# A recurrent attention block and its feed-forward layer: two rounds by halves of the features, and one product by seven for eight twice

## The chip, the cores and the metric

The kernel runs on one core of a Trainium2 chip. The metric is device time in microseconds (us), the median of several runs. All data are 32-bit floats, except that the two weight matrices arrive as 64-bit floats.

## The reference

```
# x: 8 batches x 8 heads x 512 tokens x 64;  state: 8 x 8 x 32 x 64
scores  = x @ state^T / 8 ;  a  = softmax(scores) ;  xread = a  @ state     # per batch and head
scores2 = state @ x^T / 8 ;  a2 = softmax(scores2);  sread = a2 @ x
t = concat([xread, sread], tokens)         # 4352 rows (8 x 544) x 512 features (8 heads x 64)
h = t @ w_in                               # 512 x 2048
g = h * erf(softplus(h))
out = g @ w_out                            # 2048 x 512
```

## The kernel before

**Attention.** Each of the 8 batches has an attention: scores of 512 tokens against 32 states, both softmaxes, with 32x32 turns on DVE. The weights of tokens are turned through 16 small DMAs from SBUF to SBUF (`send`, L360: `sc<-xT`), and the product `read_tokens` (L275) gives the states' reading of the tokens. `xread` is never formed: the states are multiplied with `w_in` first (`mixed_pair`, L383: `h<-w_in,st`), and the hidden layer is the product of that with the softmax weights `aT`.

**Products by seven for eight.** Both large products are cut in 2 x 2 blocks and made by seven block products instead of eight, with sums of blocks on DVE ahead of them and of results behind. `hidden_wide` (L469 to L520) makes the hidden layer of one batch in passes of 256 columns (L489); its results leave PSUM through copies on ACT and sums on DVE. `project_wide` (L620 to L667) makes the second product (L641), 256 columns a pass. Batch 0 is an exception: its products are plain, 512 columns wide (L919 and L926), while the weights are still arriving and are being turned from 64-bit to 32-bit floats on ACT and DVE (`weight`, L143 to L175).

**Order.** After batch 0, the loop at the end of the kernel takes batches 1 to 7, and for each two steps `u`, one per half of the 2048 features. In each step the second product of what the step before made runs between the pieces of the hidden product. `w_in` lies in SBUF by halves; the other half comes back from a copy in DRAM (`bring`, L1108, 2 MB a batch). The first half's output goes out by plain stores on the SP queue (L706), the second half's is added in DRAM by accumulating stores on POOL's queue (L704). The 256 rows of states come last (`hidden_states`, L534: 128 columns a pass; `project7`, L616; `store7`). The order of batch 0 and the start is a list of names (`order0`); after it, the order in which the code issues things. `in_order` (L81) then binds each engine to that order.

Of the kernel before, what the change touches and what calls it, by code (L numbers as in the profile page):

```python
# [15 lines left out]

@with_exitstack
def kernel(
# [8 lines left out]

# [8 lines left out]
    NF = d_ff // P  # L44
    GF = 4
    NG = NF // GF
    TB = S + Ns
    scale = 1.0 / (D ** 0.5)
    assert NI * Ns == P and 2 * D == P and d_model == H * D and S == 512 and NI == NK
    assert (B * Ns) % P == 0 and B * Ns <= S  # L50

    const = ctx.enter_context(tc.tile_pool(name="const", bufs=1))
    xin = ctx.enter_context(tc.tile_pool(name="xin", bufs=1))
    att = ctx.enter_context(tc.tile_pool(name="att", bufs=1))
    small = ctx.enter_context(tc.tile_pool(name="small", bufs=2))
    keep = ctx.enter_context(tc.tile_pool(name="keep", bufs=2))
    mix = ctx.enter_context(tc.tile_pool(name="mix", bufs=4))
    act = ctx.enter_context(tc.tile_pool(name="act", bufs=2))
    outs = ctx.enter_context(tc.tile_pool(name="outs", bufs=2))
    ps_at = ctx.enter_context(tc.tile_pool(name="ps_at", bufs=2, space=PSUM))  # L60
    ps_h = ctx.enter_context(tc.tile_pool(name="ps_h", bufs=2, space=PSUM))
    ps_o = ctx.enter_context(tc.tile_pool(name="ps_o", bufs=1, space=PSUM))

    ident = const.tile([P, P], F32, name="ident")
    make_identity(nc, ident)

    ring = const.tile([P, 2, 3, GF, GF, P], F32, name="ring")
    dram = ctx.enter_context(tc.tile_pool(name="dram", bufs=1, space=bass.MemoryType.DRAM))
    x_t = {}


    def load_x(b):
        t = xin.tile([P, NC, H, D], F32, name="x")
        for h in range(H):
            nc.sync.dma_start(out=t[:, :, h, :], in_=x[b, h].rearrange("(c p) d -> p c d", p=P))
        x_t[b] = t

    def traced():
        return len(nc.cur_bb.bb.instructions)

    def in_order(begun, engines=(nc.tensor, nc.vector, nc.scalar, nc.sync)):  # L81

        last = {}
        for i in nc.cur_bb.bb.instructions[begun:]:
            if i.engine in last:
                tc.add_manual_dep(i, last[i.engine].name, mybir.DependencyInfo(
                    mybir.DependencyClass.NoSync, mybir.DependencyReason.DATA), reason="in_order")
            if i.engine in [e.engine for e in engines]:
                last[i.engine] = i

    begun = traced()

    xq_t = {}

    def load_xq(b, hs=range(H)):
        if b not in xq_t:
            xq_t[b] = xin.tile([P, NI, S // Ns, Ns], F32, name="xq")
        t = xq_t[b]  # L100
        for h in hs:
            i, e = h // 2, h % 2
            for k in range(2):
                nc.sync.dma_start(
                    out=t[D * e + Ns * k:D * e + Ns * k + Ns, i],
                    in_=x[b, h, :, Ns * k:Ns * k + Ns].rearrange("(m t) d -> t m d", t=Ns))


    st = const.tile([P, B, P], F32, name="st")
    away0 = ring[:, 1, 0].rearrange("p k i t -> p (k i t)")  # L110
    st0 = away0[:, 512:640].rearrange("p (g d) -> p g d", g=2)
    x0 = xin.tile([P, NC, H, D], F32, name="x").rearrange("p c h d -> p (c h d)").rearrange(
        "p (h c d) -> p h c d", h=H, c=NC)
    x_t[0] = x0.rearrange("p h c d -> p c h d")
    for i in range(NI):
        (nc.scalar, nc.sync)[i % 2].dma_start(
            out=x0[:, 2 * i:2 * i + 2].rearrange("p h c d -> p h (c d)"),
            in_=x[0, 2 * i:2 * i + 2].rearrange("h (p c) d -> p h (c d)", c=NC))
        if i == 1:
            nc.sync.dma_start(out=st0, in_=state[0].rearrange("(g h) n d -> (h n) g d", g=2))  # L120

    def load_st(hs):
        for h in hs:
            i, e = h // 2, h % 2
            nc.sync.dma_start(out=st[Ns * i:Ns * i + Ns, 1:B, D * e:D * e + D],
                              in_=state[1:B, h].rearrange("b n d -> n b d"))


    w_in = const.tile([P, NF // 2, NK, P], F32, name="w_in")
    away = ring[:, :, 2].rearrange("p u k i t -> p u (k i t)").rearrange(  # L130
        "p u (j k f) -> p u j k f", k=NK, f=P)
    of_group = [w_in[:, GF * g:GF * g + GF] for g in range(2)] + [away[:, u] for u in range(2)]
    pieces_in = [of_group[j // 2][:, 2 * (j % 2):2 * (j % 2) + 2] for j in range(NF // 2)]
    kept_in = dram.tile([2, P, NF // 2, NK * P], F32, name="kept_in")
    w_out = const.tile([P, NF, d_model], F32, name="w_out")

    fetched = []

    def weight(dst, src, parts=1):

        flat = lambda t: t.rearrange("p a b c -> p (a b c)" if len(t.shape) == 4 else
                                     "p a b -> p (a b)")
        if src.dtype == F32:
            fetched.append(nc.sync.dma_start(out=dst, in_=src))
            return [lambda: None] * 2 * parts, [lambda: None] * 3 * parts
        raw = act.tile([P, 2 * 2 * d_model], U32, name="raw", bufs=3)  # L150
        blocks = [(raw, src)]
        if len(src.shape) == 4:
            blocks = [(raw.rearrange("p (h x) -> p h x", h=2)[:, h], src[:, h]) for h in range(2)]
        for to, part in blocks:
            part = part.bitcast(U32)
            fetched.append(nc.sync.dma_start(
                out=to.rearrange("p (a b) -> p a b", a=part.shape[1]), in_=part))
        n, m = dst.shape[1] // parts, d_model // parts * 4
        on_act, on_dve = [], []
        for k in range(parts):  # L160
            to, words = dst[:, n * k:n * k + n], raw[:, m * k:m * k + m]
            words = words.rearrange("p (n w) -> p n w", w=2)
            lo, hi, to = words[:, :, 0], words[:, :, 1], flat(to)
            d = to.bitcast(U32)
            on_act += [
                lambda to=to, hi=hi: nc.scalar.activation(out=to, in_=hi.bitcast(F32),
                                                          func=ACTF.Copy, scale=2.0 ** -112),
                lambda lo=lo: nc.scalar.activation(out=lo, in_=lo, func=ACTF.Copy,
                                                   scale=2.0 ** -29)]
            on_dve += [  # L170
                lambda d=d: nc.vector.tensor_scalar(d, d, 3, None, op0=ALU.logical_shift_left),
                lambda on=nc.vector, d=d, lo=lo: on.tensor_tensor(d, d, lo, op=ALU.add),
                lambda d=d, hi=hi: nc.vector.scalar_tensor_tensor(
                    out=d, in0=hi, scalar=0x80000000, in1=d, op0=ALU.bitwise_and,
                    op1=ALU.bitwise_or)]  # L175
        return on_act, on_dve

    gw = GF * P

    def weights_in(j):  # L180
        return weight(pieces_in[j], moe_w_in[:, 2 * P * j:2 * P * j + 2 * P].rearrange(
            "(k p) (h f) -> p h k f", p=P, f=P), 2 if j == 0 else 1)

    def weights_out(j):
        return weight(w_out[:, 2 * j:2 * j + 2, :],
                      moe_w_out[2 * P * j:2 * P * j + 2 * P].rearrange("(t p) e -> p t e", p=P))

    leads = [0]

    def warm(out, n, by=ident):  # L190
        for _ in range(n):
            nc.tensor.matmul(out=out, lhsT=by, rhs=by, start=True, stop=True)

    def lead(out):

        warm(out, leads[0])
        leads[0] = 0

    sT = const.tile([P, NK, 2, Ns, B // 2], F32, name="sT")
    st00 = away0[:, 768:1024]  # L200
    where = {h: (g, q) for g, hs in enumerate(((0, 2, 1, 3), (5, 7, 4, 6)))
             for q, h in enumerate(hs)}
    aT = {}

    def all_of(jobs):
        for f in jobs:
            f()

    over = lambda t: t.unsqueeze(2).to_broadcast([P, NC * NI, Ns])

    def inverse(z):
        nc.vector.tensor_scalar(z, z, 1e-9, None, op0=ALU.add)
        nc.vector.reciprocal(z, z)

    marks = []

    def scored(b, xT, pool=ps_at, names=("at", "at")):


        s2 = [pool.tile([P, S], F32, name=name) for name in names]  # L220
# [8 lines left out]
    def scores(b, xT, *pool):  # L229
# [3 lines left out]
        for e in range(2):  # L233
            last = nc.scalar.copy(sc[:, e], s2[e])
# [30 lines left out]
    def read_tokens(b, a2T, z2, pool=ps_at, name="at"):  # L265
# [14 lines left out]
        if z2 is None:  # L280
            return lambda on: on(sn, sr)
# [1042 lines left out]
```

## Time and profile before

| | |
|---|---|
| median of 3 runs | 722.42 us (721.96 to 723.0) |
| span of the profiled execution | 720.8 us |
| that execution's own time | not given apart from its span; the median stands 1.6 us above the span |
| PE busy | 714.0 us, 99% |
| DVE busy | 489.0 us, 68% |
| ACT busy | 420.9 us, 58% |
| DMA moved | 74.65 MB, mean 104 GB/s |
| share of PE in the chain that ended last | 97% |

The profile has one execution of the program. PE is TensorE's matmuls, PEld its weight loads, DVE is VectorE, ACT ScalarE, POOL GpSimd, SP SyncE; a `q` behind an engine is its DMA queue. A group's line has source line, engine, operation, what is written and read, shapes, count, busy us and mean ns of one, and the idle time of the engine ahead of it. L numbers are lines of the kernel before.

### The profile page before, as it was taken

Reading aid. Unit: us, or ns where it says so; the run is one execution under the profiler, and the core shown is the slowest. Engines: PE = TensorE matmul, PEld = TensorE weight load, DVE = VectorE, ACT = ScalarE, POOL = GpSimd, SP = SyncE. Lnnn points to the kernel's source line nnn. Section 1 sums busy time; section 2 is a strip of 40 time slices with the busy share of each in tenths; the row PEclk is TensorE's granted clock in tenths of the full one; section 3 lists DMA queues with packets and bytes.
Section 4 is the critical chain, followed back from the end, with each engine's and each line's share of the span. In section 5 each row is a group of like instructions: output and inputs, shape, how many; then the busy total and the mean of one; then the engine's idle time right before and its main releaser. Section 6 shows DMA issues by size and latency. Waiting matters only on the chain.

```text
span 720.8 us, 10926 instructions
## 1 busy us (share of the span) xinstructions
PE 714.0 (99%) x4291; PEld 558.4 (77%) x4291; DVE 489.0 (68%) x796; ACT 420.9 (58%) x619; POOL 25.2 (3%) x34
## 2 busy tenths in 40 slices
PE   8999999999999999999999999999999999999997
PEld 7444347688878878787888878787888888889996
DVE  6998886869767875768575766577575736555533
ACT  4999897657474627564566547472666545452340
POOL 0000000000100000000000000000000000000000
PEclk9999999999999999999999999999999999999999
DMA  8879686650348172514523280615142322002100
GB/s 253 238 206 245 220 239 192 152 156 30 56 93 205 26 145 35 163 34 107 77 43 136 58 146 0 176 31 148 29 121 67 100 35 30 31 29 30 22 9 30
DMA packets 144068, 74.65 MB, mean 104 GB/s; under 512 B 123024, under 2 KB 132624, under 8 KB 142480
## 3 DMA queue, kind: packets, MB, share of 16 engines
q1 hardware_dynamic: 139152, 65.89, 33.6%
q0 software_dynamic: 4032, 7.34, 7.6%
q8 instruction: 34, 0.56, 0.3%
q10 hardware_dynamic: 832, 0.72, 0.3%
q14 instruction: 18, 0.15, 0.1%
HBM read 49.81 MB, written 20.45 MB: 97 GB/s over the span
## 4 chain that ended last, share of the span: by engine, by line
PE 97%; DMA 2%; ACT 0%; issue 0%; SPq 0%; DVE 0%
PE o L641 47%; PE h L489 17%; PE o L926 8%; PE at L489 7%; PE h L534 3%; PE o L616 3%; PE at L919 2%; PE h L919 2%; PE h L383 2%; DMA raw<-in_moe_w_out_dram 2%; PE at L383 2%; PE at L275 1%; PE o L224 1%; PE at L908 1%; DMA x<-in_x_dram 1%; PE at L1018 0%
## 5 line engine op out<-in xcount | busy, mean ns | idle before, releaser
L641 PE MATMUL o<-w_out,ring 128*128 128x256 f32 x896 | 203.0, 379 | 0.0
L641 PEld LDWEIGHTS o<-w_out,ring 128*128 128x128 f32 x896 | 169.8, 190 | 24.9 <-DVE ring L1127 0.8
L641 PE MATMUL o<-raw,ring 128*128 128x256 f32 x672 | 161.4, 381 | 0.0
L641 PEld LDWEIGHTS o<-raw,ring 128*128 128x128 f32 x672 | 126.5, 190 | 25.9 <-ACT m L385 9.2
L472 DVE TENSOR_TENSOR ring<-ring,at 128x512 f32<-128x512 f32 x56 | 38.2, 682 | 86.6 <-ACT ring L510 79.5
L482 ACT ACTIVATE ring<-ring 128x512 f32<-128x512 f32 x112 | 70.6, 631 | 20.1 <-DVE ring L472 19.1
L489 PE MATMUL h<-aT,m 128*128 128x256 f32 x336 | 81.8, 379 | 0.0
L1127 DVE TENSOR_TENSOR ring<-ring 128x1024 f32<-128x1024 f32 (+1 forms) x61 | 70.7, 1201 | 4.5 <-ACT ring L546 4.5
L489 PEld LDWEIGHTS h<-aT,m 128*128 128x128 f32 x336 | 63.8, 190 | 10.0 <-issue 1.2
L926 PE MATMUL o<-w_out,ring 128*128 128x512 f32 x128 | 59.5, 599 | 0.0
L626 DVE TENSOR_TENSOR ot<-uv,o 128x256 f32<-128x256 f32 (+1 forms) x56 | 31.0, 553 | 37.7 <-PE o L641 35.9
L664 ACT COPY ot<-o 128x256 f32<-128x256 f32 x28 | 10.4, 372 | 77.9 <-PE o L641 77.9
L704 POOL DMA_DIRECT2D out_dram<-ot x28 | 24.5, 943 | 656.6 <-DVE ot L626 557.0
L926 PEld LDWEIGHTS o<-w_out,ring 128*128 128x128 f32 x128 | 23.7, 190 | 28.1 <-issue 26.6
L626 DVE TENSOR_TENSOR ot<-ot,o 128x256 f32<-128x256 f32 x56 | 22.1, 416 | 27.8 <-ACT ot L664 27.7
L673 DVE TENSOR_TENSOR ring<-ring 128x512 f32<-128x512 f32 x56 | 38.6, 689 | 1.4
L674 DVE TENSOR_TENSOR ring<-ring 128x512 f32<-128x512 f32 x56 | 36.1, 684 | 0.0
L385 ACT COPY m<-h 128x512 f32<-128x512 f32 x13 | 7.6, 586 | 46.3 <-PE h L383 46.1
L506 ACT COPY ring<-h 128x512 f32<-128x512 f32 x28 | 16.4, 585 | 29.6 <-PE h L489 29.6
L501 ACT COPY ring<-h 128x512 f32<-128x512 f32 x28 | 16.4, 586 | 28.0 <-PE h L489 25.5
L489 PE MATMUL h<-sy,m 128*128 128x256 f32 x112 | 31.0, 399 | 0.0
L489 PE MATMUL h<-sy,sx 128*128 128x256 f32 x112 | 30.9, 398 | 0.0
(205 smaller groups left out, 994.9 us busy)
## 6 DMA issues: line engine op xcount, KB each, us to landing
w_in<-kept_in SPq DMA_DIRECT2D x7, 2048.0 KB, 8.8
out_dram<-ot SPq DMA_DIRECT2D x33, 256.0 KB, 2.2
raw<-in_moe_w_in_dram SPq DMA_DIRECT2D x16, 512.0 KB, 5.4
raw<-in_moe_w_out_dram SPq DMA_DIRECT2D x8, 1024.0 KB, 5.8
xq<-in_x_dram SPq DMA_DIRECT2D x112, 64.0 KB, 3.2
x<-in_x_dram SPq DMA_DIRECT2D x56, 128.0 KB, 3.2
out_dram<-ot POOLq DMA_DIRECT2D x28, 256.0 KB, 4.6
sc<-xT SPq DMA_DIRECT2D x112, 32.0 KB, 1.9
```

What stands on the lines that cost most here:

```text
L383: nc.tensor.matmul(out=ps[k][e][q, :], lhsT=st[r, b, q], rhs=of_group[g][r, :, i, :], start=True, stop=True)
L472: add = lambda o, x, y: nc.vector.tensor_tensor(o, x, y, op=ALU.add)
L482: nc.scalar.activation(out=s[k], in_=hs[k], func=ACTF.Softplus)
L489: nc.tensor.matmul(out=out[:, i], lhsT=x[:, q:q + P], rhs=y, start=(first and i == 0), stop=(i == 1), skip_group_check=not first)
L626: add = lambda o, x, y: tt(o, x, y, op=ALU.add)
L641: nc.tensor.matmul(out=out, lhsT=lhs[:, i, :], rhs=rhs[:, g, i, :], start=(start and i == 0), stop=(i == GF - 1), skip_group_check=not start)
L673: return [lambda: tt(S1, A21, A22, op=ALU.add), lambda: tt(S2, S1, A11, op=ALU.subtract), lambda: tt(S3, A11, A21, op=ALU.subtract), lambd ...
L674: lambda: tt(S3, A11, A21, op=ALU.subtract), lambda: tt(S4, A12, S2, op=ALU.subtract)]
L704: nc.gpsimd.dma_start(out=rows[2 * h + r][:, c], in_=ot[:, c], accum_op=ALU.add)
L919: nc.tensor.matmul(out=h_t[g, i], lhsT=m_t[0, g][:, e, P * i:P * i + P], rhs=aT[0][:, e], start=start, stop=not start)
L926: nc.tensor.matmul(out=acc[r], lhsT=gT[g][:, i, P * r:P * r + P], rhs=w_out[:, GF * g + i, :], start=(made_of[r] == 1), stop=(made_of[r] = ...
L1127: nc.vector.tensor_tensor(s[:, ks], s[:, ks], hs[:, ks], op=ALU.mult)
```

## The change

The kernel is rewritten around the same operations.

- **Two rounds.** Round A runs batch 0 (plain, first half of the features) and batches 1 to 7 with the first 1024 features; round B runs batches 0 to 7 with the other 1024. The 256 state rows lie between the rounds (first half) and inside the start of round B (second half). All attentions fall into round A.
- **Kept softmax weights.** Each batch's `y` (the turned softmax weights of the first softmax) and their block sums `sy` go to DRAM in round A (`yk`, `yl`) and come back in round B (`yK`, `yL`).
- **Kept weights.** The second halves of `w_in` and `w_out` are converted during round A into DRAM and brought back once (`wi`, `wo`).
- **Second product in round A**: seven block products of 256 columns, in the form that adds inside PSUM (`second`), two groups of 128 rows each.
- **Second product in round B** (`second_twice`): seven for eight twice. Each of the seven block products is itself made by seven smaller ones, so 49 of them, 98 matmuls of 128 columns a batch. DVE makes the sums of quarters of the activations (`inner_sums`, on 4 and on 3 of the seven at once); the sums of quarters of the weights are made once (`twice`). Its four results go out by accumulating stores on POOL's queue; `res`, one buffer of 7 x 512 a partition, holds them and the first four results of the smaller products.
- **Batch 7 of round B** (`second_last`): it loads round A's output, adds on DVE, and writes by plain stores; one of the seven is made whole.
- **One listed order.** A string `ORDER` names all 2400 steps, DMA issues included; they are issued in that order, and `in_order` binds each engine, SP and POOL too. A name like `~7*11` is eleven warming matmuls into bank 7.
- In the names, `A3...` is batch 3 of round A, `B3...` of round B, `a3...` its attention: `a3s` scores, `a3xq`/`a3x` loads, `a3z` the 16 turning DMAs, `rd3` the reading product, `rn3`, `rt3`, `rc3` what follows it. `f0`, `f1` are the two halves of the hidden product, `e`, `g` erf and multiplication, `A1` to `A4` block sums of activations, `p` the second product, `d` stores.

The core of the diff:

```diff
-from collections import deque
+ORDER = """
+warm lx0 lst0 lx2 lx1 lx3 i0l0 lst8 lst5 lst3 lst7 lst4 lst1 ~7*11 x0 lst2 s0 lst6 x0c i1l1 x2 s0c
...
+a5z01 A5M3 a5z00 y52 a5z31 A5f05 a5iy A5M2 a5x2 a5x6 y54 A5f02 A4A1 a5z11 A5f06 a5z02 a6xq4 y53
...
+a5z10 o6v1 A5f0s22 a5z33 A5f03 A5f0c21 A3d1 a6tx2 yk5 A4p60 A5f0s12 o7l1 A5f0c12 A5f1c A3d0 a6tx1
+A5f0s21 A4A4 A5f16 rd5 A5e0 A5f15 rn51 a6x7 rn50 a6tx3 A4p61 A5f1u2 rt5
...
+"""
-    def project_wide(n, g, put, more):
...
-        yield from product(A11, B11, a, True)
-        nc.scalar.copy(m1, a)
...
+    def second(u, w, slot, nh, store):
+        P_, Q_, R_ = (b[:, 0:E2 * nh] for b in bank[3:6])
...
+        products(1, P_, True)
+        step(n("pc"), act.copy, Q_, P_)
+        products(5, R_, True)
+        products(6, Q_, False)
+        step(n("pu2"), act.copy, o[1], Q_)
...
+    def inner_sums(g, t, k0, k1):
+        s1, s2, s4 = (l2[:, k0:k1, k] for k in range(3))
+        q11, q21, q12, q22 = (quarter(t[:, 1 + k0:1 + k1], o, h)
+                              for o in range(2) for h in range(2))
+        step(g + "1", add, s1, q21, q22)
+        step(g + "2", sub, s2, s1, q11)
+        step(g + "3", sub, q21, q11, q21)
+        step(g + "4", sub, s4, q12, s2)
...
+                for i in range(2):
+                    pe.matmul(out=out_[:, P * j:P * j + P], lhsT=lhs[:, i], rhs=rhs[:, i],
+                              start=(start and j == 0 and i == 0), stop=(i == 1),
+                              skip_group_check=True)
...
+        step(g + "u2", act.copy, quad(0, 1), four(Q_))
...
+    def second_twice(u, w, slot, store):
+        ws = w.seven()
+        inner_sums(u + "a", ring[slot], 0, 4)
+        inner_sums(u + "b", ring[slot], 4, 7)
+        inner(u + "a", ws, slot, range(0, 4), bank[3:6], res[:, 0:4])
+        step(u + "C11", add, res[:, 1], res[:, 1], res[:, 0])
+        step(u + "d0", store, 0, 0, res[:, 1])
+        inner(u + "b", ws, slot, range(4, 7), bank[3:6], res[:, 4:7])
+        step(u + "U2", add, res[:, 4], res[:, 4], res[:, 0])
...
+        step(u + "C2", add, res[:, 2:4], res[:, 2:4],
+             res[:, 5].unsqueeze(1).to_broadcast([P, 2, 512]))
+        step(u + "d2", store, 1, 0, res[:, 2])
+        step(u + "d3", store, 1, 1, res[:, 3])
...
-    in_order(begun, [nc.tensor, nc.vector, nc.scalar])
+    for name in ORDER.split() or do:
+        if name[0] == "~":
+            k, n = name[1:].split("*")
+            issue(name, lambda: warm(bank[int(k)][:, 0:P], int(n)))
+        else:
+            issue(name, do.pop(name) if ORDER.split() else do[name])
+    in_order(begun)
```

The quoted rows of `ORDER` are parts of it, with line breaks moved.

## The prediction

> **What bounds the kernel now.** I read the page first: span, busy shares, granted clock and the summary of the chain.
>
> ```profile
> span 720.8 us, 10926 instructions
> PE 714.0 (99%) x4291; PEld 558.4 (77%) x4291; DVE 489.0 (68%) x796; ACT 420.9 (58%) x619; POOL 25.2 (3%) x34
> PEclk9999999999999999999999999999999999999999
> PE 97%; DMA 2%; ACT 0%; issue 0%; SPq 0%; DVE 0%
> ```
>
> TensorE sets the time: 97% of the chain that ended last is its own work, at a full granted clock. So the price of the change is first a count of matmul passes (an f32 matmul of the program is two passes in the trace). The mean duration of one pass is no price, since passes overlap. The chain of waits in order of time (start, length, what) gives the pitch of long runs.
>
> ```profile
> 28.98 10.30 PE o L926 x24
> 163.50 12.09 PE o L641 x56
> 255.99 1.02 PE h L383 x16
> 655.73 3.57 PE h L534 x32
> ```
>
> A pass of 512 columns costs 10.30 / 24 = 0.429 us, of 256 columns 12.09 / 56 = 0.216, of 128 columns 3.57 / 32 = 0.1116. Sixteen of the small mixing passes cost 1.02. Next, the groups by shape, for the weight loads, and the timeline of DVE:
>
> ```profile
> L641 PEld LDWEIGHTS o<-w_out,ring 128*128 128x128 f32 x896 | 169.8, 190 | 24.9 <-DVE ring L1127 0.8
> L534 PE MATMUL h<-sy,m 128*128 128x128 f32 x64 | 7.8, 275 | 0.0
> 48.70 1.28 DVE L961 TENSOR_TENSOR ring<-ring,h 128x512 f32<-128x512 f32 x2
> 701.40 2.36 DVE L1127 TENSOR_TENSOR ring<-ring 128x1024 f32<-128x1024 f32 x2 [3.92 <-ACT ring L546]
> ```
>
> The reader sees that back-to-back DVE operations also overlap: two of 512 take 1.28 us where one takes 0.68, so the pitch is 0.60; for 1024 it is 2.36 - 1.22 = 1.14. Last, the issue of DMAs, which the change crowds: SP's timeline, then the lines of the turning DMAs and of the accumulating stores (min/median/max).
>
> ```profile
> 256.05 5.57 SPq L75 DMA_DIRECT2D x<-in_x_dram  x8
> 261.71 10.49 SPq L104 DMA_DIRECT2D xq<-in_x_dram  x16
> 315.32 10.41 SPq L360 DMA_DIRECT2D sc<-xT  x16
> L360 SPq DMA_DIRECT2D sc<-xT x112: 586/609/1888, 111.8 to 562.7; - x112
> DMA to landing us min/median/max: 1.9/1.9/7.0
> L704 POOL DMA_DIRECT2D out_dram<-ot x28: 862/862/1218, 184.5 to 681.5; - x28
> DMA to landing us min/median/max: 3.9/4.6/6.8
> ```
>
> On SP a turning DMA ("z") costs 10.41 / 16 = 0.65 us, a token load ("x") 0.70, a quarter of the xq loads 0.66.
>
> **The products.** Before, one batch of tokens takes 336 passes of 256 columns (two halves of 56 hidden and 112 second): 72.5 us. After, round A takes 56 + 112 passes, 36.3 us, and round B 56 of 256 columns (12.1) and 196 of 128 (21.9): 70.3, so 2.3 less for each of batches 1 to 6, 13.8 in all. Batch 0 was plain: 64 + 128 passes of 512, 82.5 us; now half of that, 41.2, and one unit of round B, 34.0: 7.3 less. Batch 7 keeps one of its seven products whole (8 of 256 and 16 of 128, 3.5 us, for 28 of 128): 1.9 less. The states are recast without a change of count. Products: -23.0.
>
> **The rest of TensorE.** Sixteen more mixing matmuls, 32 passes: +2.0. Batch 0 mixes 32 fewer of 256 columns, which overlap like the others: -1.0 (between 0 and -2). Warming matmuls, 48 for 30: +4.0 at most (nothing, if they stand where PE would wait; the list puts them before its first hidden product, where they fill waits of the start; I count them). TensorE in all: -18.0.
>
> **DVE and ACT** must hide beside this. A unit of round A asks DVE for 20 attention operations (12.0 us at 0.60), 4 mixing and 4 hidden sums and 2 second sums (6.0), 2 multiplications of 2048 (4.6), 4 sums of 1024 (4.6), the sums of y (1.4), one piece of weights (2.9) and small ones (0.8): 32.3 of TensorE's 40.4 us. A unit of round B asks for 28.3 of 36.0: the new sums of quarters cost 4.6 + 3.5 of it. Both are under TensorE's time, so I cost them at nothing; the cover is 8 us a unit, and if it went (an operation of DVE waiting at the head of its queue) each us beyond it would be a us. At the start DVE, ACT and PE are nearly level for 60 us; 0 to +3 there, I take 0 as the start before had its own waits.
>
> **SP and the six readings.** This is where I expect the gain to go. Round A now has an attention per 40 us instead of per 79. Each ends in 16 z DMAs, then `rd`, the reading product, at the head of PE's queue; behind it stand the hidden and second products, and rn on DVE. For batch 5 the list has on PE, from the first z to rd5, eight hidden steps (0.86 each) and three second ones (1.73): 12.1 us, with the rest of the one running 12.1 to 13.8. On SP stand 16 z, two x, one xq step and a store: 10.4 + 1.4 + 1.3 + 0.4 = 13.5 us, and 1.9 until the last lands: 15.4. PE waits 1.6 to 3.3 us. Batches 1 to 6 have the same make-up (11.5 to 13.5 us of SP against 10.4 to 12.1 of PE, plus up to 1.7); batch 7 has 20 us and no wait. I take 1.7 each, the near end, as DVE can run ahead: +10.2, between 0 and 22.
>
> **The stores of round B.** `res` has one buffer: the copy u2 of the next unit waits for the last two accumulating stores, with 6.3 to 7.3 us of PE work listed between. The row says 4.6 to landing, 6.8 at most: 0, as 4.6 is the nearest; but a store has twice as many and half as long runs now, and if its issue took 1.7 and landing 6.8, 1.2 for each of seven units: 0 to +8.6.
>
> **State and y kept in DRAM, w_in and w_out brought once:** beside PE work of 10 us or more each, where 2 MB took 8.8 to land: 0. **The end:** after the last product seven DVE steps (3.7), issue and landing (2.6) follow, where before 3.7 us went by: +2.6.
>
> **Sum:** -18.0 + 10.2 + 2.6 = -5.2 against the profiled span of 720.8, which stands 1.6 under the median of 722.4 (launch and end); 722.4 - 5.2 = 717.2.
>
> **Two rules of the Trainium skill.** The row first: 128-column passes with a new 128x128 load each ran every 0.1116 us, so loads hide. The page "TensorE: Matmul & The Clock Gate" (Part 3, what overlaps) says loads overlap running matmuls only in different row groups, which 128-row operands never have; with its 107 ns per load the 1540 narrow passes would cost an estimated 165 us more, and the trace disagrees. The other: granted clock is full in every slice, and the first 16 matmuls at the start, cold, took 429 ns against 281 warm. The same page (Part 1, HAM) halves the clock after an idle window of about 3.4 us; by that rule waits of 1.7 us are free and longer ones cost an estimated 1.7 us again each; no run here shows it yet.
>
> **Rivals.** *The readings are hidden* (DVE's shorter pitch lets the z start 2 us earlier): -18.0 + 2.6, 707.0. For it: the list leaves PE no visible hole. Against: SP's 0.65 is measured back to back. *Slower: the z land late.* Loads of weights, stores and kept states now share the DMA engines with them (the trace's own xq and x take 3.2 to land). At 4.0 instead of 1.9 each of the six reads waits 3.8: -18.0 + 22.8 + 2.6, 729.8. It decides from 2.8 us to landing, where six waits of 2.6 eat the gain. *The narrow products don't run at half the time:* at the 190 ns of one load per pass, 1540 x 0.078 = +121, 838; the L534 run speaks against it.
>
> **How the numbers follow.** Forecast 0.40, hidden readings 0.23, late landings 0.33, narrow pitch 0.04. A measurement tells 0.2% (1.4 us) from no change. The forecast's own range is 711 to 723: 0.30 faster, 0.08 same, 0.02 slower. Hidden readings are all faster; late landings 0.03 same, 0.30 slower; the last is slower. Faster 0.53, same 0.11, slower 0.36. The range runs from 704 (hidden, with the warming free) to 732 (late landings, with some of the stores).
>
> **What would show it.** Narrow passes at 0.11 us in the chain; PE idle before the reading line, released by a2T's DMAs, six times 1.7; ACT's u2 never waiting on POOL's stores; SP's z at 0.65. Wrong if PE idles elsewhere (on ACT copies or DVE) by more than 5 us in sum, or not at all at the readings.

## The result: no gain, and the profile after

In one comparison the changed kernel took 723.78 us (median of 10, 722.02 to 725.25) and the kernel before 722.02 (median of 10, 721.25 to 723.0): a ratio of 1.0021, 95% interval 1.0012 to 1.0031. It is slower by 1.8 us, where 5.2 less was forecast. The profiled execution spans 721.9 us, 1.1 more than before; the sum had 720.8 - 5.2 = 715.6.

The page of the kernel after, with the lines that answer to those of before (span, busy time, granted clock, chain by engine):

```profile
span 721.9 us, 12570 instructions
PE 703.9 (98%) x5027; PEld 584.9 (81%) x5027; DVE 555.3 (77%) x749; ACT 475.7 (66%) x711; POOL 37.6 (5%) x38
PEclk9999999999999999999999999999999999999999
PE 73%; SPq 10%; DVE 6%; DMA 3%; ACT 2%; issue 2%; DVEq 0%
```

TensorE lost 10 us of busy time, but the chain that ended last is no longer its own: 97% became 73%, and a tenth of the chain is SP issuing DMAs. Where SP enters is seen in the chain of waits in order of time (start, length, what). First the first reading, then a long run of the narrow passes:

```profile
82.58 0.61 SPq L534
83.19 0.04 issue
83.23 1.92 DMA at<-at
85.15 0.73 issue
85.88 1.07 PE b L467 x58
...
87.84 2.44 PE b L493 x16
...
673.72 30.82 PE b L734 x276
```

L534 is a turning DMA, L467 the reading, L493 the scores behind it, L734 the narrow product. The last turning DMA lands 1.92 us after its issue and releases the reading. The narrow passes take 30.82 / 276 = 0.1117 us, as forecast. The longest of PE's own waits (us in total, times, longest):

```profile
PE b L467 <- DMA at<-at: 6.6, 7, 1.6
```

The lines of the turning DMAs and of the accumulating stores (issue in ns, min/median/max):

```profile
L534 SPq DMA_DIRECT2D at<-at x112: 585/608/1263, 72.0 to 321.2; - x112
L651 POOL DMA_DIRECT2D out_dram<-res x32: 886/1197/2212, 440.7 to 701.5; - x32
```

The turning DMA costs what was forecast; a store's issue rose from 0.86 to 1.20 us, and its median landing is 4.5 us behind the issue.

The recorded waits at the readings make 6.6 us, 10.2 were forecast; they are not the whole price, as the windows around the first reading show (each row: start and end, length, then busy us and instructions of PE, PEld, DVE, ACT and POOL, PE's granted clock, DMA share, GB/s):

```profile
84.00:86.00 2.00, 0.64 (x14) 0.34 (x17) 1.30 (x2) 1.99 (x2) 0.00 (x0) 1.00 0.44 118
86.00:88.00 2.00, 1.43 (x60) 1.05 (x57) 1.02 (x3) 0.49 (x2) 0.00 (x0) 1.00 1.03 356
88.00:90.00 2.00, 2.00 (x16) 0.23 (x14) 2.00 (x2) 1.97 (x3) 0.00 (x0) 0.50 0.95 248
```

Behind the wait the clock was halved for some 3 us (0.50 in the last row, 0.64 in the window after it), and the 16 scores took 2.44 us. The best measure of round A is therefore the time from the first pass of the first reading to the first pass of the seventh, six units of work. It and the rest, for the kernels that follow (us, from PE's timeline of each profiled execution; the last column is the median of the timed runs):

| kernel | reading 1 | reading 7 | between | from there to the end | span | median |
|---|---|---|---|---|---|---|
| after | 83.73 | 326.32 | 242.6 | 395.6 | 721.9 | 723.8 |
| x loads on POOL (e2) | 83.09 | 319.32 | 236.2 | 395.5 | 714.8 | 718.5 |
| half of the turning DMAs (e3) | 83.67 | 315.36 | 231.7 | 395.9 | 711.3 | 713.5 |
| turning DMAs in 1 KB runs (e5) | 83.92 | 320.95 | 237.0 | 395.7 | 716.6 | 718.3 |
| e2 and e5 together (e6) | 83.25 | 317.65 | 234.4 | 395.6 | 713.2 | 716.0 |
| warming ahead of reading 1 (e8) | 86.49 | 327.72 | 241.2 | 395.3 | 723.0 | 726.2 |
| turned weights via DRAM (e9) | 84.08 | 315.76 | 231.7 | 395.4 | 711.2 | 713.0 |

Everything behind reading 7 (round A's last unit, states, round B) takes 395.3 to 395.9 in all of them.

### The profile page after: what moved, and what is told of

It reads as the page before. It is cut to its first block, busy times and chain, and to the rows that moved or that the text cites. A ratio compares the mean times of both kernels' runs of the same rounds, so it can differ in the third digit from the quotient of the medians.

```text
span 721.9 us, 12570 instructions
## 1 busy us (share of the span) xinstructions
PE 703.9 (98%) x5027; PEld 584.9 (81%) x5027; DVE 555.3 (77%) x749; ACT 475.7 (66%) x711; POOL 37.6 (5%) x38
## 4 chain that ended last, share of the span: by engine, by line
PE 73%; SPq 10%; DVE 6%; DMA 3%; ACT 2%; issue 2%; DVEq 0%
PE b L734 24%; PE b L623 17%; PE b L675 17%; SPq L534 7%; PE b L926 3%; PE b L575 3%; PE b L886 2%; PE b L865 2%; DMA at<-in_x_dram 2%; DMA at<-at 2%; PE b L467 1%; DVE at L238 1%; PE b L493 1%; SPq L298 1%; SPq L303 1%
## 5 line engine op out<-in xcount | busy, mean ns | idle before, releaser
L675 PE MATMUL b<-ta,ring 128*128 128x256 f32 x840 | 193.1, 381 | 0.0
L675 PEld LDWEIGHTS b<-ta,ring 128*128 128x128 f32 x840 | 158.0, 191 | 31.7 <-issue 9.2
L238 ACT COPY ring<-b 128x512 f32<-128x512 f32 (+1 forms) x138 | 79.8, 584 | 87.3 <-PE b L623 60.8
L623 PE MATMUL b<-y,m 128*128 128x256 f32 x480 | 120.1, 382 | 0.0
L238 ACT COPY res<-b 128x512 f32<-128x512 f32 (+2 forms) x104 | 54.5, 532 | 83.9 <-PE b L734 41.0
L623 PEld LDWEIGHTS b<-y,m 128*128 128x128 f32 x480 | 88.1, 191 | 16.0 <-issue 2.2
L232 DVE TENSOR_TENSOR ring<-ring 128x2048 f32<-128x2048 f32 (+1 forms) x36 | 77.7, 2166 | 28.0 <-ACT ring L631 23.0
L623 PE MATMUL b<-sy,m 128*128 128x256 f32 x360 | 91.2, 382 | 0.0
L734 PEld LDWEIGHTS b<-at,ring 128*128 128x128 f32 x660 | 79.8, 192 | 5.0 <-ACT res L238 1.1
L734 PE MATMUL b<-at,ring 128*128 128x128 f32 x660 | 82.3, 276 | 0.0
L231 DVE TENSOR_TENSOR ring<-ring 128x1024 f32<-128x1024 f32 (+2 forms) x67 | 75.3, 1132 | 0.1
L238 ACT COPY m<-b 128x512 f32<-128x512 f32 (+2 forms) x65 | 35.4, 565 | 16.5 <-PE b L575 16.1
L238 ACT COPY b<-b 128x512 f32<-128x512 f32 (+2 forms) x57 | 31.3, 553 | 20.3 <-PE b L623 9.3
L238 DVE STREAM_TRANSPOSE at<-at 128x512 f32<-128x512 f32 x56 | 38.6, 700 | 3.0 <-DMA at<-in_x_dram 1.2
L734 PE MATMUL b<-cv,ta 128*128 128x128 f32 x312 | 40.2, 276 | 0.0
L734 PEld LDWEIGHTS b<-cv,ta 128*128 128x128 f32 x312 | 38.1, 192 | 1.3 <-issue 0.8
```

The source lines that it names most:

```text
L231: sub = lambda o, a, b: tt(o, a, b, op=ALU.subtract)
L232: mul = lambda o, a, b: tt(o, a, b, op=ALU.mult)
L238: do[name] = lambda: f(*args)
L623: pe.matmul(out=to[:, i], lhsT=xs[n - 1][:, q:q + P], rhs=ys[n - 1], start=(start and i == 0), stop=(i == 1), skip_group_check=True)
L675: pe.matmul(out=to[:, E2 * h:E2 * h + E2], lhsT=a[:, k // 2, k % 2], rhs=rhs[n][:, k], start=(start and h == 0 and k == 0), stop=(k == 3), ...
L734: pe.matmul(out=out_[:, P * j:P * j + P], lhsT=lhs[:, i], rhs=rhs[:, i], start=(start and j == 0 and i == 0), stop=(i == 1), skip_group_ch ...
```

## The experiments

Theory: six readings wait because SP's line ahead of them (16 turning DMAs and what stands between) is longer than PE's work. Rival: the attention's steps on DVE and ACT are late and the DMAs only close the loop. What the runs are held against is the kernel after, 723.8; the kernel before took 722.0 to 722.5 in every comparison.

**e3: half of the turning DMAs left out.** In `ORDER`, the eight z of each attention whose two numbers have an odd sum are gone.

> Eight of the 16 turning DMAs of each attention are left out, so half of a2T keeps older values; the price of the other eight on SP is read from it. Theory (SP's issue): as with two queues, without any cost on ACT: 709 to 714. Rival (loop through DVE): 720 to 724.

713.47 (ratio to before 0.9875, 0.9862 to 0.9888): 10.3 less. PE has no wait at any reading, and the six units take 231.7. The rival is out: with the same work on DVE and ACT no loop was late.

**e4: eight of them issued twice.**

```diff
+                if (mm + i) % 2:
+                    do[name("z%d%dr" % (mm, i))] = do[name("z%d%d" % (mm, i))]
```

> Eight of the 16 turning DMAs of each attention are issued twice, right behind each other: the dose upwards. Theory (SP's issue is on the path in all of batches 1 to 6): 5.2 us for each of six readings, +31, and something at the seventh: 750 to 760. Rival (loop through DVE with slack on SP): 723 to 730.

845.81 (1.1707, 1.1691 to 1.1722), 122 more, four times what the theory said. The dose was another than intended: a repeat writes the same place, so at SP's head it waits for the landing of the first. In the chain most pairs have a landing of 1.9 in them, about 2.5 us a pair with an issue: SP's line grows by some 8 x 2.5 = 20 us a reading. PE waits 15 to 17 us at each of the seven readings, 113.7 in all where the kernel after had 6.7; so a longer line ahead of a reading is paid for nearly in full. The rest of the 122 came with the clock, which was 0.92 in the mean where the kernel after had 0.996. Most of the waits are in the waits view's first line:

```profile
PE b L469 <- DMA at<-at: 88.2, 10, 17.3
```

**e1: half of them on ACT's queue.**

```diff
-                step(name("z%d%d" % (mm, i)), lambda mm=mm, i=i: nc.sync.dma_start(
+                eng = nc.scalar if (mm + i) % 2 and b in (1, 2, 3, 4, 5, 6, 7) else nc.sync
+                step(name("z%d%d" % (mm, i)), lambda mm=mm, i=i, eng=eng: eng.dma_start(
```

> Eight of the 16 turning DMAs of each attention are issued on ACT's queue, eight stay on SP's. Theory (SP's issue sets the readings): 8 x 0.65 = 5.2 us less on SP between the last turn on DVE and the landing, more than the waits of 1 to 4.8 us; PE's wait on a2T goes to nothing and the time from 723.8 to between 711 and 715, minus what ACT loses. Rival (the attention's loop through DVE and ACT is late and the DMAs only close it): the wait moves to the next step of the loop, 720 to 724. Second rival (ACT's copies are held up by its DMAs, 8 x 0.65 us of ACT a unit and a wait at its head): 724 to 735.

732.62 (1.0129, 1.0114 to 1.0144), the second rival. The chain ahead of the second reading shows why (L624 hidden products, L238 ACT's copy, L298 an x load, L535 a turning DMA):

```profile
118.52 0.88 PE b L624 x4
...
119.47 0.02 ACT ring L238
119.50 2.38 DMA at<-at
...
121.89 0.45 SPq L298
...
122.38 0.59 SPq L535
```

ACT issues in its own order, so its last two turning DMAs stood behind a copy that waited for PE until 119.5; then an x load on SP waited for their landing, with three more turning DMAs behind it. Half the issues were moved to a queue that waits for the very engine they hold up.

**e2: the loads of tokens on POOL's queue.**

```diff
-        nc.sync.dma_start(out=x_n[:, :, h, :], in_=x[b, h].rearrange("(c p) d -> p c d", p=P))
+        nc.gpsimd.dma_start(out=x_n[:, :, h, :], in_=x[b, h].rearrange("(c p) d -> p c d", p=P))
```

> The loads of tokens (x, eight an attention, 0.65 us each on SP) are issued on POOL's queue, which is empty in round A. Theory (SP's issue): two of them stand between the turning DMAs and some wait for the reading at SP's head ahead of the quarters for the next scores, so 1 to 2 us of each of the six waits go: 712 to 719. Rival (loop through DVE): 722 to 725. Rival (POOL's issue is slow and the loads land late): above 725.

718.54 (0.9942, 0.9928 to 0.9955). POOL took 0.75 us for an issue (56 of them), and they land at leisure; the six units take 236.2, 6.4 less.

**e11: the same relief by order alone.** In `ORDER`, SP's DMAs between the first and the last z of an attention go behind the last z.

> The kernel after with one change of order: of SP's DMAs, those that stand between the first and the last turning DMA of an attention (two x, an xq, a store or a kept piece: 2 to 4 of 0.4 to 0.65 us) go behind the last. Theory (the length of SP's line ahead of the reading): 1.5 to 2 us less at each of six readings; the wait for the next scores gets them back only in part: 714 to 720. Rival (SP's whole work sets the pitch of a unit, so order is worth nothing): 722.5 to 725.

732.38 (1.0127, 1.0112 to 1.0143). The edit was bad in two ways. In batches 5 and 6 it also put a quarter (xq) behind the turn that reads it, so that these two turn older data; and the x moved are those that the same reading needs. PE now waits for them at the readings (3.9 us in four waits); x takes 3.2 us to land, a turning DMA 1.9. The run says nothing for or against the theory.

**e5: the same DMAs in runs of 1 KB.** The turn on DVE writes its 32x32 blocks in the order in which they are sent:

```diff
-            step(name("ty%d" % e), turn, both[:, e], both[:, 2 + e])
+            step(name("ty%d" % e), turn, blocks[:, :, e].rearrange("p m c n -> p c m n"),
+                 both[:, 2 + e].rearrange("p (c m n) -> p c m n", c=NC, n=Ns))
...
-                    out=rows[Ns * mm:Ns * mm + Ns, i], in_=blocks[Ns * i:Ns * i + Ns, mm]))
+                    out=at[Ns * mm:Ns * mm + Ns, 7168 + 256 * i:7424 + 256 * i],
+                    in_=at[Ns * i:Ns * i + Ns, 4096 + 256 * mm:4352 + 256 * mm]))
```

> The turned weights of tokens are laid out by blocks, so that each of the 16 turning DMAs of an attention moves 32 runs of 1 KB in place of 256 runs of 128 bytes; count, bytes, order and queue stay (one turn on DVE of batch 5 stands one step later). Theory (SP's issue sets the readings, and its price goes with the runs: 128 runs of 4 KB took 0.48 us for a kept y): pitch from 0.65 to 0.3 to 0.45, 3 to 5.6 us less a unit, the reading waits vanish as when half of them were left out: 711 to 716. Rival (SP's pitch is one price for each DMA, whatever its runs): 722 to 725.

718.29 (0.9949, 0.9934 to 0.9963), but not for the reason given. The line of the turning DMAs shows that the issue hardly fell, 588 ns for 608:

```profile
L535 SPq DMA_DIRECT2D at<-at x112: 507/588/1230, 71.7 to 315.2; - x112
```

PE's waits at the readings went from 6.6 to 3.5 us:

```profile
PE b L467 <- DMA at<-at: 3.5, 5, 1.0
```

For these two shapes SP's price is nearly one for each DMA; on that point the rival was right, though its 722 to 725 was not. The small difference still counts: from the first of the 16 issues to the end of the last, SP's line is 0.5 to 0.8 us shorter at each of the six readings, 3.5 in all. Of the 5.6 won between readings 1 and 7, 2.6 lie in the first unit (36.46 for 39.02 from reading 1 to 2): the first wait was 0.74 in place of three gaps, and the clock stayed at 1.00 from 80 to 100 us. The other units won 0 to 1.2 each.

**e6: e5 and e2 together.**

> The runs of 1 KB and the loads of tokens on POOL's queue together. Theory (both are one cause, the length of SP's line ahead of the reading): they do not add up, since after the first there is no wait left to take: 709 to 714. Rival (two causes: the turning DMAs late for the reading, the quarters of the next scores late behind them): they add, 705 to 710.

715.99 (0.9908, 0.9895 to 0.9921). Between readings 1 and 7 it takes 234.4, where each alone took 236.2 and 237.0, and the two gains would have added up to 230.6. That is less than the 231.7 of e3, where no reading waits; so of 10.9 that could be won, e6 won 8.2, and the gains overlap, as the theory said. But the median is above its range, and two waits (0.9 and 0.5 us) were left.

**e9: by way of DRAM**, in five DMAs for 16, with e2's loads and e5's order of blocks; the five stand at the places of the first five or six of the 16:

```diff
+        step(name("zs"), lambda: nc.sync.dma_start(out=kept_z[b], in_=at[:, 4096:5120]))
+        for mm in range(NI):
+            step(name("zr%d" % mm), lambda mm=mm: nc.sync.dma_start(
+                out=at[Ns * mm:Ns * mm + Ns, 7168:8192].rearrange("t (i x) -> t i x", i=NI),
+                in_=kept_z[b].rearrange("(i t) (m x) -> m t i x", i=NI, m=NI)[mm]))
```

> The turned weights go to DRAM in one store (128 runs of 4 KB) and come back in four loads of 128 runs of 1 KB, five DMAs on SP in place of 16; the loads of tokens are on POOL's queue. Theory (the length of SP's line ahead of the reading): 5 x 0.5 + 3.2 to landing + 2 to landing, 7 to 8 us in place of 12 to 15, and 7 us less of SP a unit: no wait at any reading, as when half of the turning DMAs were left out (711.3 profiled, 713.5): 711 to 714.5. Rival (two landings in a row cost more than 16 issues): 717 to 724.

712.99 (0.9867, 0.9854 to 0.9881), inside the theory's range. SP's timeline of one attention:

```profile
220.55 0.34 SPq L529 DMA_DIRECT2D kept_z<-at  x1
223.19 1.73 SPq L531 DMA_DIRECT2D at<-kept_z  x4
```

The loads start 2.64 us behind the store's issue, take 1.73 to issue and 2.9 to land: 7.3 us, though the data go out and come back. No reading waits, and the six units take 231.7, what they took with half of the DMAs left out. So 721.9 - 711.2 = 10.7 us of the span is the price of the readings.

**e8: warming matmuls ahead of the first reading.** `~7*14` stands before `rd1` in `ORDER`.

> The kernel after with 14 warming matmuls into a free bank right ahead of the first reading, where PE waits and where the granted clock fell to 0.50 and 0.64 for 4 us behind the wait. Theory (the gap takes the clock): the clock stays at 1.00 in 84 to 96 us and 1 to 2.5 us are saved, 721 to 723. Rival (the fall has another cause, and the matmuls take the place of waiting): the clock falls all the same, 723 to 726.

726.17 (1.0047, 1.003 to 1.0064). The window behind the wait, with the clock full:

```profile
88.00:90.00 2.00, 1.78 (x17) 0.45 (x17) 2.00 (x3) 1.40 (x2) 0.00 (x0) 1.00 0.96 235
```

From reading 1 to 2 it is 35.5 for 39.0, so the gap did take the clock. But the reading began 2.8 later, behind the matmuls, and the units from reading 5 to 7 took 2.1 more (85.9 for 83.8). PE waits 2.1 us at reading 6 where it waited 1.5, and the clock is halved behind that wait (0.50 from 286 to 288). With SP's line unchanged, what PE won at one reading it lost at a later one.

**e7: without 27 warming matmuls.** `~4*16`, `~6*6` and `~7*5` are gone from `ORDER`.

> The kernel after without 27 of its 40 listed warming matmuls, the three groups between batch 0's attention and its first second products. The prediction's step (they cost what they take, 27 passes-pairs of about 0.15 us): 4 us less at most, 720 to 722. Rival (they stand where PE waits for converted weights): 723 to 725, no change. Second rival (without them the granted clock falls in the waits of the start): 725 to 735.

728.50 (1.0081, 1.0065 to 1.0098), 4.7 more, the second rival. PE's timeline shows it standing 3.87 us at a stretch:

```profile
19.69 1.11 PE L407 MATMUL b<-ident,ring 128*128 128x128 f32 x4 [3.87 <-DVE ring L230]
```

and the windows show the clock at 0.50 from there to 28; the first of them:

```profile
20.00:22.00 2.00, 2.00 (x10) 1.66 (x8) 2.00 (x4) 1.20 (x3) 0.00 (x0) 0.50 1.08 365
```

So the warming stands where PE would wait, and without it the clock falls; the forecast had counted it as a cost. But the fall at the start is not the whole price. In this profiled execution (span 728.4, the slowest of its runs) reading 1 is only 1.3 us later than in the kernel after; the other 5 us come between readings 3 and 5, where PE waits 1.6 and 2.6 us for the turning DMAs (0.5 and 1.6 in the kernel after) and the clock is halved again behind both waits. How the start moved those readings was not followed.

**e10: the end.** Seven of batch 7's last sums are cut in two, the halves that are ready first placed where DVE waits:

```diff
+        ends = lambda t: t.rearrange("p (q c) -> p q c", c=P)[:, 0:4:3]
+        mid = lambda t: t.rearrange("p (q c) -> p q c", c=P)[:, 1:3]
...
+            step(u + n + "e", add, ends(o), ends(a), ends(b_))
+            step(u + n, add, mid(o), mid(a), mid(b_))
```

> The kernel after, where seven of batch 7's last sums on DVE (128x512, 0.6 us each) are cut in two halves of 256 columns; the halves of the first and last quarter, whose products are done earlier, are placed where DVE waits for PE, 4 to 6 us before the end. Theory (the end is DVE's line behind the last product, 6.5 us from the last pass to the end of the span against 3.7 before): 7 x 0.29 = 2 us less, 721 to 722.5. Rival (the end is set by the last stores' landing): 723 to 725.

723.04 (1.001, 1.0001 to 1.0018), 0.7 less for 2 expected, at the edge of the rival's range. DVE's timeline shows a wait that the halves did not take away:

```profile
714.00 1.03 DVE L229 TENSOR_TENSOR ring<-ring,res 128x512 f32<-128x512 f32 x2 [0.98 <-ACT res L237]
```

One sum at the head of DVE's queue (C11) waits for ACT's copy of the last narrow product, with seven others behind it.

**What was still open.** With the readings free the span is 711.2, where the sum without them says 720.8 - 18.0 + 2.6 = 705.4. Three runs on top of e9: e12 moves a second product of batch 0 (`o34`) between the first reading and its turn; e13 takes e10's halves and puts C11 behind the sums that wait for nothing; e14 does both.

```diff
-i5v1 rd1 T2 A1e0 rn10 a2x0 rn11 i5v2 rt1 i6l1 rc1 a2x7 a2s A1g0 A1f1s21 o34
+i5v1 rd1 T2 A1e0 rn10 a2x0 rn11 i5v2 o34 rt1 i6l1 rc1 a2x7 a2s A1g0 A1f1s21
...
-B7U2 B7bc21 B7C11 B7q10 B7w4 B7d0 B7U3 B7C121 B7C22 B7d11 B7w5 B7d3 B7C120 B7C21 B7d10 B7d2
+B7U2 B7w4 B7U3 B7w5 B7q10 B7bc21 B7C22 B7d3 B7C11 B7d0 B7C120 B7d10 B7C121 B7d11 B7C21 B7d2
```

> On the kernel with the turned weights by way of DRAM (713.0, profiled 711.2): one second product of batch 0 (o34, 1.72 us) is moved between the first reading and the turn behind it. There PE stood 0.9 us for rn on DVE, and 16 scores behind it took 1.64 us where others take 1.09. Theory (this wait is part of what the sum lacked, and it has cover at no cost): 0.9 to 1.4 us less, 711.5 to 712.2. Rival (the step was cover elsewhere, and the wait turns up there): 712.7 to 713.5.

> On the kernel by way of DRAM: the halved sums of the last batch, and behind the last product the sums that wait for nothing come first, C11 (which waits for ACT's copy of the last narrow product) after them. In the run with halves alone DVE stood 0.98 us for that copy with six sums behind it. Theory (the end is DVE's line): 0.6 us for the halves, 1.2 for the order: 711 to 711.6. Rival (stores' landing): 712.5 to 713.5.

> Both together: they lie at opposite ends of the kernel and add up: 709.6 to 710.8. Rival (time won at the first unit is lost to a later wait of round A): 711 to 711.6, the end's share alone.

e12: 712.78 (0.987, 0.9855 to 0.9884), as e9 within the runs' spread. The wait for rn is gone, and another has come (PE for ACT's copy of a mixed piece, ahead of the second mixing product):

```profile
93.20 1.57 PE L573 MATMUL b<-w_in,st 64*32 64x512 f32 x16 [0.67 <-ACT m L233]
```

The rival was right: there is no free cover there. e13: 711.94 (0.9858, 0.9843 to 0.9873), 1.05 less for 1.8 expected, between its two ranges. e14: 711.79 (0.9856, 0.984 to 0.9873), the same as e13 and just above its rival's range. e14 is the fastest version: 1.4% under the kernel before, and some 12 us under the kernel after.

## Why the prediction was wrong, step by step

**Products and the rest of TensorE: right as a count.** The passes of both kernels, counted at the pace of their back-to-back runs, make 708.1 before and 688.7 after: 19.4 less, for 18.0 in the sum. Narrow passes ran at 0.1117.

**The readings: right in place and sum, wrong in make-up.** 10.7 us by e9, for 10.2. But it is not 1.7 six times: PE's recorded waits were 1.4, 0.3, 0.5, 1.6, 1.5 and 1.5, some 6.6 in all. PE's weight loads, which the waits view lists apart, waited 8.6 for the same landings. The clock, halved for 3.4 us behind the first reading, took an estimated 1.7 (half of that): together 10.3. The rival of late landings fell: a turning DMA landed in 1.9.

**The first step that failed is the start, "0 to +3, I take 0".** "At the start DVE, ACT and PE are nearly level for 60 us" was the reading of the trace; the value taken did not follow from it. Before, the first reading (batch 0's) began at 74.15, 4.3 us behind the count of passes ahead of it; in e9 reading 1 (batch 1's) at 84.08, 6.9 behind: +2.6. The first unit, 1 to 2, then takes 35.8 for a count of 33.7, where the next five take 0.7 more than their count each: 1.4 again. PE waited 5.2 us in all until 87 us, 3.1 before:

```profile
PE b L852 <- DVE w_in L346: 1.8, 2, 1.3
PE b L474 <- DVE sn L472: 0.9, 1, 0.9
PE b L884 <- DVE ring L227: 0.8, 1, 0.8
```

These are the longest of e9's waits: all are for DVE. The one move that was tried, e12, won nothing. So the start and first unit cost 4.0 by this count; measured up to the reading of batch 2 in both kernels, it is 2.4.

**The second is a price: "Sixteen of the small mixing passes cost 1.02".** The sum took it for both kernels alike, and put at nothing that the order now scatters these passes. Before, most of them stand in blocks of 32, or of 48 with the next scores behind a reading (first view; PE's timeline). In e9 they stand in 34 blocks of 16 behind reading 1 (second view).

```profile
255.92 1.09 PE L383 MATMUL h<-w_in,st 64*32 64x512 f32 x16
256.80 1.06 PE L383 MATMUL at<-w_in,st 64*32 64x512 f32 x16
257.66 1.06 PE L224 MATMUL o<-xq,st 64*32 64x512 f32 x16
```

```profile
204.84 3.62 PE L673 MATMUL b<-ta,ring 128*128 128x256 f32 x16
208.38 1.09 PE L573 MATMUL b<-w_in,st 64*32 64x512 f32 x16
209.40 0.92 PE L673 MATMUL b<-ta,ring 128*128 128x256 f32 x3
```

By their starts, sixteen passes with more of their kind behind them take 0.88 and 0.86 us. Sixteen that stand alone take 1.02, and the change into them 0.09 more (3.54 from 204.84 to 208.38, where 16 passes of 256 columns make 3.45). Added up over the starts of all passes behind the first reading, the small ones (mixing, scores, readings) take 5.0 us more against their count than before, the first unit's share left out; changes between other passes take 2.0 less. This is read from the two traces; no run joined the blocks again.

**The end: +2.6 forecast, 2.7 measured** in the kernel after (6.4 us from the end of the last pass to the end of the span, 3.7 before). By e13 one us of it was DVE's halves and order.

**DVE and ACT in the rounds, the stores, the kept states: 0, right.** In e9 no wait of PE behind 87 us is recorded; the stores cost ACT waits (3.8 us in round B), PE none, although POOL's issue rose from 0.86 to 1.2 us.

**The account.** Without readings the sum said 705.4, e9 spans 711.2: 5.8 more. The count of passes was 1.4 better; start and first unit cost 4.0; the end was 0.2 less in e9 than taken. 3.4 us are left: behind the first reading, time exceeds the count of passes by 9.4 in e9 and by 4.7 before, and 1.4 of the difference is the first unit's. They are spread over 620 us, and the scattered small passes make 3.0 of them (5.0 - 2.0). With the readings 0.5 dearer, 5.8 + 0.5 = 6.3 is the whole miss. The signs that the prediction named did not show it: outside the readings PE's recorded waits for DVE make 4.1 us in the kernel after, under the 5 named, and passes at a slower pitch leave no idle time in the profile.

**The rival of hidden readings (707.0)** named a condition that e9 made true, and e9 is at 713.0. It had the same holes.

**The rule on the clock.** The page "TensorE: Matmul & The Clock Gate" of the Trainium skill (Part 1, HAM) has the clock halve after an idle window of about 3.4 us. e7 agrees: a gap of 3.87 us, and the clock at 0.50 behind it. The kernel after shows more than the prediction made of the rule: behind gaps of 0.31, 1.05 and 0.57 us with some 60 tiny passes between them the clock was halved as well, while single waits of 1.5 us at readings 4 to 6 left it at 1.00. So waits under 1.7 us were not free where little work lay between.

## What to carry to other kernels

Where a change makes a short loop of several engines run twice as often, add up the line of the queue that closes it: here SP's 16 issues of 0.6 us cost the kernel 10.7 us, and five larger DMAs that go through DRAM and back beat them. Price a small product as it stands in the order: sixteen mixing passes cost 1.1 us alone and 0.9 within a block. Put an issue on a queue that waits for nothing (POOL), not on one that waits for the engine you want to free (ACT). Where three engines are read as level, take the cost from the upper part of the range, not 0.

## What the runs showed of the hardware that was not expected

- Between partitions, an issue on SP was priced by the DMA, hardly by its runs: 0.608 us for 256 runs of 128 bytes, 0.588 for 32 runs of 1 KB. In e9 the store to DRAM took 0.34 and a load back 0.43, so other shapes have another price. The page "DMA: Bandwidth & Descriptors" of the Trainium skill (SWDGE vs HWDGE vs iDMA, on issuing engines) calls the time to initiate a DMA usually small beside the DMA. Here 16 issues took about 10 us and the last landing 1.9, so the trace disagrees for these DMAs of 32 KB.
- A store to DRAM and four loads back took some 7.3 us, less than 16 direct copies between partitions.
- In e4 a DMA that writes where the one ahead of it is still under way was held at the head of the queue until that one had landed: 2.5 us for each repeated pair.
